# Two-scale attention with a gated convolution: 64-bit weights decoded in other passes and on another engine, one step's coarse scores from raw K, and another opening order

## The chip, the cores and the metric

One core of one Trainium2 chip. The metric is device time in microseconds (us) of one run of the whole program. Engines are named as in the profile: PE (TensorE, matmuls; PEld its weight loads), DVE (VectorE), ACT (ScalarE), POOL (GpSimd), SP (SyncE, which issues most DMAs). Each engine works through its own list of instructions in order, and waits where an instruction's inputs or buffers are not ready.

## The reference

```python
# B=8, H=8, S=576, D=64, factor 4; all in fp32
q_d, k_d, v_d = (mean of 4 neighbours along S of q, k, v)      # 144 rows
out_d  = softmax(q_d k_d^T / 8) v_d                            # coarse attention
out_up = repeat(out_d, 4)
local  = softmax(mask(|i-j| < 4, q k^T / 8)) v                 # banded attention
x = (out_up + local) as (B, S, 512)
# second half: weights come as float64
gate = sigmoid(sum_k conv_w[k] * x shifted by 4-k)             # 5 taps, causal
out  = (gate * (x @ w_val)) @ w_out
```

## The kernel before

**Steps.** The attention runs in 16 steps (`i`), two pairs of heads each (`p = 2i, 2i+1`; 32 pairs in all). A step has these pieces on PE: `sla`, `slb` (local scores, tile `sl`), `sd` (coarse scores), `odp` (coarse weights times V, into tile `x`), `xa`, `xb` (local weights times V, into the same `x`). Between them stand on DVE and ACT: `mx` (row maxima of `sl`), `sub`, `exp`, `sum`, `norm`, `turn` (transpose), `spr` (four copies of 32 partitions into `pt`); for the coarse part `cmx0`, `cexp`, `cnorm`, `cturn`. `oc` copies the coarse result out on ACT, and `xu`, `xt` add both parts into the tile `xt` on DVE.

**Projections.** `xh` and `xl` split `xt` into two parts of fp32r (tiles `xhs`, `xls`), and the product with `w_val` (tile `val`) is made of three matmuls for each of four slices (pieces of 3 matmuls, by blocks `j` of 504 columns). `tap4` and `tap0` to `tap3` make the convolution in tile `gp`, `gate` its sigmoid, `h` the product with `val`; `hhi`, `hlo` split `h` (tile `hhl`), and the product with `w_out` is the tile `out`.

**PSUM.** Scores and `x` share three buffers (`AB`). They are handed round in PE's order: the second `x` tile of step 1 takes the buffer of step 2's `sl`, which `sub` of step 2 frees (line 733).

**Coarse inputs.** For the first two batches (`SUMB`) the sums over 4 neighbours of q and k are made on the chip (`qe`, line 672); later ones by DMAs that add while they land, issued by POOL (`qs`, `vs`, line 585: an issue waits until the one before it has landed). The V sums of the first batch are added from four loads (`vr0` to `vr3`, tiles `vs` and `raw`; `va`, `vc`, `vb`, line 605).

**Weights.** Each of eight chunks (4 of `w_val`, 4 of `w_out`; 128 x 512 float64, tile `raw_v`, `raw_o`) is loaded, then decoded to fp32: three passes on ACT (lines 1007 to 1009), one on DVE (`val`, line 1012), then split into `wh` (ACT, 1036) and `wl` (DVE or POOL, 1039):

```python
nc.scalar.activation(out=low, in_=lo, func=AF.Copy, scale=LOW)                                  # uint16 out
nc.scalar.activation(out=top, in_=hi, func=AF.Prelu, scale=2.0**-40, alpha=2.0**100)            # int16 out
nc.scalar.activation(out=hi, in_=hi, func=AF.Copy, scale=2.0**-112)                             # fp32 out
```

**The order.** A planner in the kernel lists all operations with a cost for each engine that may do them, gives each a due time from PE's order (`tensor_order`), runs a list schedule over these costs, and writes the instructions out in the order of their planned starts. `EARLY` fixes the order of the first loads on SP, `PACE` and `TURN` how PE mixes steps and projections.

Of the kernel before, what the change touches and what calls it, by code (L numbers as in the profile page):

```python
# [12 lines left out]
U16 = mybir.dt.uint16  # L13
# [101 lines left out]
class Transfers:  # L115


    ALONE = {"SP": 0.30, "POOL": 0.16}
    SHARED = {"SP": 0.15, "POOL": 0.128}
    FIRST = {"SP": 1500, "POOL": 1950}  # L120
    LANDING = 1600
# [33 lines left out]
class Planner:  # L155
# [293 lines left out]
def tensor_order():  # L449
# [29 lines left out]
    some("sla slb sd", 0)  # L479
    some("sla slb sd", 1)  # L480
    some("odp xa xb", 0)
    proj(2)
    some("odp xa xb", 1)
    proj(4)
    some("sla slb", 2)
    proj(2)
    some("sd", 2)
    proj(2)
    for s in range(2, NSTEP):
# [10 lines left out]
def tile_two_scale_attn_gated_conv(  # L500
# [183 lines left out]
    def local_scores(i):  # L684
# [315 lines left out]
    def f64_parts(src):  # L1000
# [15 lines left out]
        return fields, value, hi  # L1016

    def weight_chunk(q, nm, w, d):
# [9 lines left out]
        def fields():  # L1028
            t["f"] = f64_parts(t["raw"])
            t["f"][0]()  # L1030

        def value():
            t["f"][1]()
# [8 lines left out]
        op(("fld", q), "ACT", 1700, fields, [("raw", q)])
        op(("val", q), "DVE", 600, value, [("fld", q)], port=ALONE)
        op(("whi", q), "ACT", 530, hi, [("val", q)])
        op(("wlo", q), either(600, 1230), 0, lo, [("whi", q)], port=BOTH)
# [236 lines left out]
```

## Time and profile before

| | |
|---|---|
| median of 3 runs | 375.66 us (374.57 to 375.9) |
| the profiled execution: time, span | 376.08 us, 373.9 us |
| busy: PE, DVE, ACT, POOL | 340.2, 309.7, 251.7, 99.4 us |
| mean granted clock of PE | 0.968 |
| PE busy of 0 to 75 us, of 75 to 300 us | 47.3 us, 222.3 us |

PE's busy time holds the filler matmuls that the kernel puts into gaps (line 558), and runs longer where the granted clock is low. Between span and time lie 2.2 us that are no part of the profile.

### The profile page before, as it was taken

To read this page: it belongs to the slowest core of one execution; us is meant where nothing else is said; L and a number is where in the kernel's file an instruction comes from. 1 tells how busy PE (TensorE), PEld (TensorE's weight loads), DVE (VectorE), ACT (ScalarE), POOL (GpSimd) and SP (SyncE) were. 2 spreads that over 40 slices of the span, in tenths; PEclk is the share of its full clock that TensorE was granted. 3 is DMA by queue.
4 is the path that set the end of the run, shared out by engine and by line. 5 is a ranking of instruction groups with operands and counts; after the bars stand their busy time and mean duration, and the time that the engine had idled before them with its cause. 6 is when DMAs were issued, how large, how long until landed. Compare 5 with 4: busy or idle time off the path is not lost.

```text
span 373.9 us, 12809 instructions
## 1 busy us (share of the span) xinstructions
PE 340.2 (91%) x5517; PEld 266.7 (71%) x5517; DVE 309.7 (83%) x495; ACT 251.7 (67%) x577; POOL 99.4 (27%) x106
## 2 busy tenths in 40 slices
PE   5865725999999899999999999999999999999996
PEld 2644513777777677777777777777777778788996
DVE  6884997999889989999898999998989993937620
ACT  1379998978875779486759694967596667415421
POOL 4223532364033711152035104601450120000000
PEclk9996986799999989999999999999999999999999
DMA  7993899577999899989868996989542301102012
GB/s 220 360 355 141 266 244 309 105 201 199 322 270 273 238 210 225 307 199 246 240 208 237 230 270 163 234 238 255 160 110 85 114 2 57 55 2 85 27 49 79
DMA packets 23463, 70.95 MB, mean 190 GB/s; under 512 B 3184, under 2 KB 9584, under 8 KB 23408
## 3 DMA queue, kind: packets, MB, share of 16 engines
q1 hardware_dynamic: 17504, 52.39, 39.0%
q0 software_dynamic: 5616, 17.50, 26.9%
q8 instruction: 43, 0.70, 0.8%
q10 hardware_dynamic: 288, 0.26, 0.2%
q14 instruction: 12, 0.10, 0.1%
HBM read 60.69 MB, written 9.44 MB: 188 GB/s over the span
## 4 chain that ended last, share of the span: by engine, by line
PE 70%; DVE 17%; ACT 7%; DMA 3%; issue 2%; SPq 0%; DVEq 0%; ACTq 0%
PE out L1058 10%; PE out L1060 8%; PE out L1059 8%; PE val L1058 8%; PE val L1060 7%; PE val L1059 7%; PE x L876 6%; PE x L920 5%; DVE gp L970 5%; PE sd L798 4%; PE sl L706 4%; DMA qk<-in_qk 3%; DVE qs L672 2%; ACT pt L763 1%; PE sl L695 1%
## 5 line engine op out<-in xcount | busy, mean ns | idle before, releaser
L970 DVE SCALAR_TENSOR_TENSOR gp<-xt,cw,gp 128x576 f32<-128x576 f32 x128 | 105.0, 855 | 5.7 <-ACT gp L964 5.4
L1058 PE MATMUL val<-xhs,wh_v 128*128 128x504 f32 (+1 forms) x160 | 63.8, 399 | 6.0 <-ACT xhs L951 6.0
L1060 PE MATMUL val<-xls,wh_v 128*128 128x504 f32 (+1 forms) x160 | 60.5, 378 | 0.8 <-POOL xls L955 0.8
L1059 PE MATMUL val<-xhs,wl_v 128*128 128x504 f32 (+1 forms) x160 | 60.1, 376 | 0.0
L1058 PE MATMUL out<-hhl,wh_o 128*128 128x504 f32 (+1 forms) x144 | 58.6, 407 | 0.0
L1060 PE MATMUL out<-hhl,wh_o 128*128 128x504 f32 (+1 forms) x144 | 55.2, 383 | 0.0
L1059 PE MATMUL out<-hhl,wl_o 128*128 128x504 f32 (+1 forms) x144 | 55.0, 382 | 0.0
L763 ACT COPY pt<-pt 32x576 f32<-32x576 f32 x64 | 42.9, 670 | 9.4 <-PE x L876 4.4
L1106 POOL TENSOR_TENSOR hhl<-h,hhl 128x504 fp32r<-128x504 f32 (+1 forms) x24 | 26.5, 1113 | 79.8 <-ACT hhl L1100 72.3
L1058 PEld LDWEIGHTS val<-xhs,wh_v 128*128 128x128 f32 x160 | 30.6, 191 | 14.3 <-ACT xhs L951 6.3
L891 DVE TENSOR_TENSOR xt<-x,od 128x288 f32<-128x288 f32 x64 | 26.6, 445 | 16.0 <-PE x L876 15.8
L1100 ACT CAST hhl<-h 128x504 fp32r<-128x504 f32 (+2 forms) x44 | 22.2, 519 | 24.6 <-DVE h L1086 24.5
L981 ACT ACTIVATE gp<-gp 128x576 f32<-128x576 f32 x32 | 21.9, 685 | 22.6 <-DVE gp L970 22.0
L1148 ACT ACTIVATE ob<-out 128x504 f32<-128x504 f32 (+2 forms) x40 | 21.7, 553 | 21.4 <-PE out L1060 16.1
L876 PEld LDWEIGHTS x<-pt,vw 64*64 64x64 f32 x1536 | 27.4, 144 | 11.7 <-issue 5.8
L1060 PEld LDWEIGHTS val<-xls,wh_v 128*128 128x128 f32 x160 | 30.4, 190 | 7.0 <-POOL xls L955 1.2
L920 PE MATMUL x<-pdt,vs 32*64 32x145 f32 x640 | 25.5, 294 | 10.2 <-DVE ex L733 7.2
L1059 PEld LDWEIGHTS val<-xhs,wl_v 128*128 128x128 f32 x160 | 30.7, 192 | 4.1
L706 PE MATMUL sl<-qk 128*24 128x60 f32 x1536 | 28.0, 221 | 6.1 <-DMA qk<-in_qk 5.6
L1058 PEld LDWEIGHTS out<-hhl,wh_o 128*128 128x128 f32 x144 | 27.1, 189 | 8.1 <-issue 2.5
L920 PEld LDWEIGHTS x<-pdt,vs 32*64 32x64 f32 x640 | 20.6, 134 | 16.3 <-issue 14.2
L706 PEld LDWEIGHTS sl<-qk 128*24 128x24 f32 x1536 | 25.8, 106 | 8.2 <-issue 4.0
(87 smaller groups left out, 638.7 us busy)
## 6 DMA issues: line engine op xcount, KB each, us to landing
qk<-in_qk SPq DMA_DIRECT2D x64, 291.0 KB, 6.5
vw<-in_vw SPq DMA_DIRECT2D x16, 768.0 KB, 6.0
qs<-in_qkr POOLq DMA_DIRECT2D x18, 576.0 KB, 7.4
out_t<-ob SPq DMA_DIRECT2D x32, 252.0 KB, 4.0
vs<-in_vgr POOLq DMA_DIRECT2D x21, 320.0 KB, 7.5
qs<-in_qkr SPq DMA_DIRECT2D x6, 576.0 KB, 6.7
vs<-in_vgr SPq DMA_DIRECT2D x7, 320.0 KB, 5.4
raw_v<-in_w_val SPq DMA_DIRECT2D x4, 512.0 KB, 7.3
```

Of the source, the lines that this page charges most:

```text
L706: nc.tensor.matmul(out=sc[32 * q : 32 * q + BQ, 2 * KW * g : 2 * KW * (g + 1)].rearrange("p (h k) -> p h k", h=2), lhsT=t[:, 1, 3 + blk : ...
L763: nc.scalar.copy(out=pt2[r, :, q % 2], in_=s["pt"][r, :, 0:BQ])
L876: nc.tensor.matmul(out=s["x", pr][r, part, 0:HALF].rearrange("p (e g j) -> p e g j", e=2, j=BQ)[:, :, g], lhsT=s["vw"][(LO, HI)[pr], n + h ...
L891: nc.vector.tensor_tensor(out=xt, in0=s["x", pr][:, part, 0:HALF].rearrange("p (e j r) -> p e j r", e=2, r=FAC), in1=od.broadcast_to([P, 2 ...
L920: nc.tensor.matmul(out=s["x", q // 2][64 * h : 64 * h + 64, 0, HALF : HALF + NG * CQ].rearrange("p (g j) -> p g j", j=CQ), lhsT=u["vs"][32 ...
L970: nc.vector.scalar_tensor_tensor(out=s["gp"], in0=s["xt"][:, k : k + S], scalar=cw[:, c, k : k + 1], in1=s["gp"], op0=ALU.mult, op1=ALU.add,)
L981: nc.scalar.activation(out=s["gp"], in_=s["gp"], func=AF.Tanh, scale=0.5)
L1058: nc.tensor.matmul(out=o, lhsT=wh[:, d, col], rhs=his[d], start=d == 0, stop=False)
L1059: nc.tensor.matmul(out=o, lhsT=wl[:, d, col], rhs=his[d], start=False, stop=False)
L1060: nc.tensor.matmul(out=o, lhsT=wh[:, d, col], rhs=los[d], start=False, stop=d == NC - 1)
L1100: nc.scalar.copy(out=t["hh"][:, cuts[n]], in_=t["h"][:, cuts[n]])
L1106: eng.tensor_tensor(out=t["hl"][:, cs], in0=t["h"][:, cs], in1=t["hh"][:, cs].bitcast(F32), op=ALU.subtract)
```

## The change

**The decode.** The three ACT passes become three operations of their own. `bits` and `power` write 32-bit words in place and may run on ACT or POOL; `sign` writes the 16-bit field on POOL. In the new order ACT does 14 of these passes over weight chunks, POOL 10.

**Raw K.** With `RAWK = (1,)` the coarse scores of step 1 (`sd`) take K unsummed: four matmuls, one for each of the 4 neighbours, add up in PSUM where one stood (80 instead of 20), and `qe` of pairs 2 and 3 sums 148 outputs instead of 432.

**Who does what.** `qe` may run on POOL as three adds (pairs 1 and 6 do); `spr` and `tap4` may run on POOL (16 of 64 and 9 of 32 do); `tap0` of pairs 0 and 1 becomes a product on ACT (`side`) and an add on POOL. `wl` of two `w_out` chunks goes from POOL to DVE, `cnorm` of two steps from DVE to ACT.

**The order.** `EARLY`, `FIRST` (PE's opening order), `PACE`, the planner's costs, and a table `SHIFT` that moves single due times. There is one buffer fewer for `gp` (`GB` 7).

```diff
-    "qk0 ql0 qk1 ql1 vr0.0:0 vr1.0:0 vr2.0:0 vr3.0:0 vw0 qk2 ql2 qk3 ql3 vr0.1:0 vr1.1:0 vr2.1:0 vr3.1:0 cwf0 raw0 raw1 vw1 raw2 raw3 qk4 ql4 qk5 ql5 vs0.1 raw4 vw2 "
-    "qk6 ql6 raw5 qk7 ql7 raw6 raw7 vw3"
+    "qk0 ql0 qk1 ql1 ql3 vr0.1:0 vr0.0:0 raw0 ql6 qk2 vr1.0:0 vr2.0:0 cwf0 raw1 qk3 ql2 vr1.1:0 vw0 raw2 qk5 vr2.1:0 raw3 qk6 vw1 raw4 vr3.1:0 ql7 raw5 ql5 "
+    "qk7 vr3.0:0 vs0.1 ql4 raw6 vw2 vw3 qk4 raw7"
...
-SUMB, RAWK = 2, ()
+SUMB, RAWK = 2, (1,)
...
-GB = 8
+GB = 7
+SIDE, SIDE2 = 2, 0
...
+FIRST = (
+    "l0 l1 sd0 sd1 p1 p1 p0 x0 p0 p1 p3 odp0 odp1 p1 sd2 l2 x1 p2 p3 p1"
+)
...
+SHIFT = (
+    "tap1:1:1 xl:7:-3 turn:4:6 val:7:1 turn:0:3 qe:5:1 bits:6:3 cturn:4:1 turn:2:6 qe:2:3 sign:5:-6 exp:4:1 sub:0:-20 gate:8:-1 hlo0.0:0:1 sum:2:6 whi:6:1 "
...
+            if lo:
+                half = s["qs"][:, 4 * SD - 2 * n :].rearrange("p (j r) -> p j r", r=2)
+                nc.gpsimd.tensor_tensor(out=half, in0=t[:, :, 0:2], in1=t[:, :, 2:4], op=ALU.add)
+                nc.gpsimd.tensor_tensor(out=out, in0=half[:, :, 0], in1=half[:, :, 1], op=ALU.add)
+                return
+            for r in range(1, FAC):
+                nc.gpsimd.tensor_tensor(out=out, in0=out if r > 1 else t[:, :, :, 0], in1=t[:, :, :, r], op=ALU.add)
...
-            op(k, "ACT", 560, spread(q), [("turn", i)], free=[("xa", i - 1), ("xb", i - 1)])
+            op(k, {"ACT": 680, "POOL": 1250}, 0, spread(q), [("turn", i)], port=("POOL",), free=[("xa", i - 1), ("xb", i - 1)])
...
-        def fields():
-            nc.scalar.activation(out=low, in_=lo, func=AF.Copy, scale=LOW)
-            nc.scalar.activation(out=top, in_=hi, func=AF.Prelu, scale=2.0**-40, alpha=2.0**100)
-            nc.scalar.activation(out=hi, in_=hi, func=AF.Copy, scale=2.0**-112)
+        def scaled(eng, t, by):
+            if eng is nc.scalar:
+                nc.scalar.activation(out=t, in_=t, func=AF.Copy, scale=by)
+            else:
+                eng.tensor_scalar(out=t, in0=t, scalar1=by, scalar2=None, op0=ALU.mult)
+
+        def bits(eng):
+            scaled(eng, lo, LOW)
+
+        def sign():
+            nc.gpsimd.tensor_scalar(
+                out=top, in0=hi, scalar1=0.0, scalar2=-32768.0, op0=ALU.is_lt, op1=ALU.mult
+            )
+
+        def power(eng):
+            scaled(eng, hi, 2.0**-112)
```

Two places in the program show the new order. Lines of the new kernel differ from those of the old: `qe` 690, `xu`/`xt` 918, `mx` 755, `cmx0` 835, `sub` 760, `sum` 769, `turn` 783, `cturn` 875, `wl` 1097, `xl` 984, V sums 622, `sign` 1062, `bits` and `power` 1056, `spr` 790, `norm` 776.

On DVE, in front of `sub` of step 2 (`ex<-sl_533` before, `ex<-sl_545` now); before:

```order
L848 STREAM_TRANSPOSE pdt_656<-pd 128x800
L1012 SCALAR_TENSOR_TENSOR raw_v_334<-raw_v_334 128x512
L970 SCALAR_TENSOR_TENSOR gp_630<-xt_82,cw,gp_630 128x576
L970 SCALAR_TENSOR_TENSOR gp_653<-xt_83,cw,gp_653 128x576
L1039 TENSOR_TENSOR wl_v<-raw_v_334,wh_v 128x512
...
L733 TENSOR_TENSOR ex<-sl_533,mx_621 128x24x30
```

and now, from the first add into `xt` of step 0 (tiles `xt_82`, `xt_83`) on:

```order
L918 TENSOR_TENSOR xt_82<-x_0_502,od_0_575 128x2x144
L783 STREAM_TRANSPOSE pt_670<-ex 128x768
L918 TENSOR_TENSOR xt_82<-x_0_502,od_0_575 128x2x144
L918 TENSOR_TENSOR xt_83<-x_0_503,od_0_579 128x2x144
L690 TENSOR_REDUCE qs_674<-qk_81 128x432
L918 TENSOR_TENSOR xt_83<-x_0_503,od_0_579 128x2x144
L755 TENSOR_REDUCE mx_714<-sl_545 128x24
L835 TENSOR_REDUCE cmx_720<-sd_684 128x5
L760 TENSOR_TENSOR ex<-sl_545,mx_714 128x24x30
```

The taps (line 970), seven of them, and the work on the weight chunk stood ahead of `sub`; now `sub` follows the adds into `xt`, one sum, and two row maxima, and all taps stand behind it.

On POOL, from the second chunk's `wl` to the split of step 0's `xt`; now (before, `wl`, `wl`, `xls`, `xls` stood here with nothing between):

```order
L1056 TENSOR_SCALAR raw_v_248<-raw_v_248 128x512
L1062 TENSOR_SCALAR raw_v_248<-raw_v_248 128x512
L1056 TENSOR_SCALAR raw_v_248<-raw_v_248 128x512
L1062 TENSOR_SCALAR raw_v_264<-raw_v_264 128x512
L622 TENSOR_TENSOR vs_123<-vs_123,raw_3_313 128x320
L622 TENSOR_TENSOR vs_123<-vs_123,raw_3_437 128x320
L602 DMA vs_449<-in_vgr 128x640
L776 TENSOR_TENSOR ex<-ex,rs_466 128x24x30
L1097 TENSOR_TENSOR wl_v<-raw_v_248,wh_v 128x512
L1097 TENSOR_TENSOR wl_v<-raw_v_264,wh_v 128x512
L698 TENSOR_TENSOR qs_674<-qk_80 128x432
L984 TENSOR_TENSOR xls<-xt_82,xhs 128x576
```

The passes over the third and fourth chunk, two of the V sums, `norm` of step 1 and the sums of pair 6 have come in ahead of `xls`, which the first product waits for. (Between the last two rows stand two more adds like the one on `qs_674`.)

## Rows read from the trace of the kernel before

**Rows 1.** Busy time by stretch: length, busy us (instructions), granted clock, DMA share, GB/s.
```profile
core 0: us, PE busy (x) PEld busy (x) DVE busy (x) ACT busy (x) POOL busy (x), PEclk, DMA share, GB/s
18.70:28.00 9.30, 5.72 (x96) 3.78 (x94) 7.75 (x12) 6.70 (x11) 2.06 (x3) 1.00 0.97 356
28.00:37.40 9.40, 5.19 (x121) 3.76 (x120) 4.43 (x8) 9.31 (x22) 3.33 (x2) 0.64 0.36 141
46.70:56.00 9.30, 2.57 (x29) 1.71 (x29) 9.30 (x13) 8.56 (x10) 3.02 (x3) 0.85 0.93 242
65.40:75.00 9.60, 9.18 (x126) 6.96 (x127) 8.86 (x15) 9.54 (x18) 3.98 (x5) 0.74 0.59 103
75.00:300.00 225.00, 222.28 (x3983) 171.97 (x3983) 210.29 (x345) 165.09 (x407) 71.15 (x70) 0.99 0.80 217
```

**Rows 2.** Timeline of PE to 84 us: start, length, line, tile, count [idle before <-releaser].
```profile
32.34 1.33 PE L558 MATMUL x<-const-bfloat16-1.0 128*128 128x350 bf16 x4 [4.21 <-ACT od L933]
...
33.59 2.79 PE L876 MATMUL x<-pt,vw 64*64 64x48 f32 x96
...
44.43 1.43 PE L798 MATMUL sd<-qs 128*32 128x144 f32 x40
...
55.21 2.68 PE L920 MATMUL x<-pdt,vs 32*64 32x145 f32 x36 [6.73 <-DVE ex L733]
...
58.88 2.16 PE L876 MATMUL x<-pt,vw 64*64 64x48 f32 x96
...
65.82 0.79 PE L1058 MATMUL val<-xhs,wh_v 128*128 128x504 f32 x1 [4.78 <-ACT xhs L951]
...
70.90 0.39 PE L1058 MATMUL val<-xhs,wh_v 128*128 128x504 f32 x1
...
83.08 0.49 PE L1058 MATMUL out<-hhl,wh_o 128*128 128x504 f32 x1
```

**Rows 3.** Timeline of DVE, 36 to 55 us.
```profile
36.50 1.55 DVE L891 TENSOR_TENSOR xt<-x,od 128x288 f32<-128x288 f32 x4 [2.13 <-PE x L876]
...
48.46 1.53 DVE L970 SCALAR_TENSOR_TENSOR gp<-xt,cw,gp 128x576 f32<-128x576 f32 x2
...
50.52 3.72 DVE L970 SCALAR_TENSOR_TENSOR gp<-xt,cw,gp 128x576 f32<-128x576 f32 x5
...
54.17 0.89 DVE L733 TENSOR_TENSOR ex<-sl,mx 128x720 f32<-128x720 f32 x1
```

**Rows 4.** ACT by form: the three passes over a weight chunk; mean ns.
```profile
L1007 ACT ACTIVATE raw_v<-raw_v 128x512 uint16<-128x512 uint32 x4 | 5.5, 1366 | 0.0
...
L1008 ACT ACTIVATE raw_v<-raw_v 128x512 int16<-128x512 f32 x4 | 5.4, 1360 | 0.1
...
L1009 ACT ACTIVATE raw_v<-raw_v 128x512 f32<-128x512 f32 x4 | 2.7, 669 | 0.1
```

**Rows 5.** Chain that ended last: the wait for the last part of step 1's scores data.
```profile
9.55 7.32 DMA qk<-in_qk
```

**Rows 6.** Tile raw_v on POOL: ns min/median/max.
```profile
L1039 POOL TENSOR_TENSOR wl_v<-raw_v,wh_v x3: 1294/1297/2077, 33.5 to 46.7; 128x512 fp32r<-128x512 f32 x3
```

**Rows 7.** POOL by form, mean ns.
```profile
L605 POOL TENSOR_TENSOR vs<-vs,raw 128x320 f32<-128x320 f32 x3 | 2.6, 863 | 2.3 <-DVE vs L605 2.2
...
L955 POOL TENSOR_TENSOR xls<-xt,xhs 128x432 fp32r<-128x432 f32 x1 | 1.1, 1140 | 0.0
...
L545 POOL MEMSET pt<- 128x1152 f32 x1 | 1.1, 1061 | 0.0
```

**Rows 8.** DVE by form, mean ns.
```profile
L672 DVE TENSOR_REDUCE qs<-qk 128x432 f32<-128x1728 f32 x8 | 15.4, 1942 | 1.9 <-DMA qk<-in_qk 1.9
```

**Rows 9.** Timeline of DVE and of POOL from 224 us, and DVE at 257.84 us.
```profile
224.40 4.01 DVE L970 SCALAR_TENSOR_TENSOR gp<-xt,cw,gp 128x576 f32<-128x576 f32 x4
...
225.37 1.70 POOL L1106 TENSOR_TENSOR hhl<-h,hhl 128x504 fp32r<-128x504 f32 x1 [11.33 <-ACT hhl L1100]
...
257.84 2.28 DVE L970 SCALAR_TENSOR_TENSOR gp<-xt,cw,gp 128x576 f32<-128x576 f32 x3 [0.70 <-ACT gp L964]
```

More of the change, by code (lines that the diff above doesn't have):

```diff
@@ L115 @@
 class Transfers:
[L118 to L121, printed above, removed]
+    ALONE = {"SP": 0.37, "POOL": 0.16}
+    SHARED = {"SP": 0.20, "POOL": 0.11}
+    FIRST = {"SP": 1200, "POOL": 1950}
+    LANDING = 1400
     def __init__(self):
@@ L168 @@
     ISSUE = {"SP": 620}
-    BEGIN = {"SP": 700, "ACT": 2450, "PE": 600, "POOL": 3000}
+    BEGIN = {"SP": 1500, "ACT": 2450, "PE": 600, "POOL": 3000}
     WINDOW = 14
@@ L252, in rank @@
             ops[k]["due"] = due
+        for word in SHIFT.split():
+            name, i, by = word.split(":")
+            if (name, int(i)) in ops:
+                ops[name, int(i)]["due"] += 1000 * int(by)
     def simulate(self):
@@ L338, in pick @@
             best = None
-            for due, k in sorted(ready[e]):
+            line = ready[e]
+            if e == "DVE":
+                line = [(due + LEAVE * ("POOL" in ops[k]["opts"]), k) for due, k in line]
+            for due, k in sorted(line):
                 if k in start or at[k].get(e, 0) > now:
@@ L477, in goal @@
                 return int(m + (n - m) * (t - a) / (b - a))
[L479 to L489, printed above, removed]
+    for word in FIRST.split():
+        name, i = word.rstrip("0123456789"), int(word.lstrip("abcdefghijklmnopqrstuvwxyz"))
+        if name == "p":
+            proj(i)
+        else:
+            some({"l": "sla slb", "x": "xa xb"}.get(name, name), i)
+    for s in range(TURNS, NSTEP):
         seen = 0
@@ L657, in pool, with add @@
         s = st[p]
-        def add():
+        def add(eng):
             u = at[p // 2]
@@ L1014, in value @@
             )
-        return fields, value, hi
+        return bits, sign, power, value, hi
     def weight_chunk(q, nm, w, d):
@@ L1026, in dma, with step, run @@
             nc.sync.dma_start(out=t["raw"], in_=w[:, d])
[L1028 to L1033, printed above, removed]
+        def step(n):
+            def run(*eng):
+                if "f" not in t:
+                    t["f"] = f64_parts(t["raw"])
+                t["f"][n](*eng)
+            return run
         def hi():
-            nc.scalar.copy(out=wh, in_=t["f"][2])
+            nc.scalar.copy(out=wh, in_=t["f"][4])
         def lo(eng):
-            eng.tensor_tensor(out=wl, in0=t["f"][2], in1=wh.bitcast(F32), op=ALU.subtract)
+            eng.tensor_tensor(out=wl, in0=t["f"][4], in1=wh.bitcast(F32), op=ALU.subtract)
         op(("raw", q), "SP", 620, dma, free=[("wlo", q - RAWB)], size=P * 512 * 8)
[L1042 to L1045, printed above, removed]
+        op(("bits", q), {"ACT": 600, "POOL": 1300}, 0, step(0), [("raw", q)], port=("POOL",))
+        op(("sign", q), "POOL", 1350, step(1), [("bits", q)], port=("POOL",))
+        op(("power", q), {"ACT": 580, "POOL": 1300}, 0, step(2), [("sign", q)], port=("POOL",))
+        op(("val", q), "DVE", 600, step(3), [("power", q)], port=ALONE)
+        op(("whi", q), "ACT", 560, hi, [("val", q)])
+        op(("wlo", q), either(600, 1300), 0, lo, [("whi", q)], port=BOTH)
         whl[nm, d] = ("wlo", q)
```

74 lines of the change are left out of this document (50 added, 24 removed), and 6 rows, old and new, of the table SHIFT.

## Prediction

> **What bounds the kernel now.** I read the busy time by stretch first. From 75 to 300 us PE is busy for 222.3 of 225 us at a granted clock of 0.99 [rows 1]: PE is the bound there, and this change takes no matmul out of it. Before 75 us it is busy for 47.3 us of 75 (the table above). So what can be won lies in the opening: how early PE comes to the point from which it never starves. As that point I take the first matmul of `val_2` of block 0, at 70.90 us [rows 2]; the PE work behind it is the same matmuls before and after.
>
> The timeline of PE then names the waits on the way there [rows 2]. The first `xa` waits 4.21 us for `oc` on ACT, until 32.34. `odp` of step 1 gets its first four matmuls out and waits 6.73 us, until 55.21, for DVE's `ex` (line 733): that is `sub` of step 2, which frees the PSUM buffer. The third piece of `val_0` waits 4.78 us for `xhs`, until 65.82. The timeline of DVE shows why `sub` came so late: seven taps stand ahead of it, from 48.46 to 54.2 [rows 3], while DVE is busy for all of 46.7 to 56 us and PE for 2.57 us [rows 1]. ACT is full from 28 to 37.4 us (9.31 of 9.4) and from 65.4 to 75 [rows 1], and 27 us of its opening are passes over weights: 8 chunks x (1.37 + 1.36 + 0.67) [rows 4].
>
> **The change part by part.** *The decode.* A pass that writes 16-bit fields takes 1.36 us on ACT, one that writes 32-bit words of the same count 0.67 [rows 4]. I price `bits` (it now writes uint32) at 0.67; its bounds are 0.67 and 1.37, since the only row with an integer output is a 16-bit one. ACT is left with 14 passes, 9.4 us in place of 27: 18 us less. [...]
>
> POOL gets 10 passes over weight chunks. No row has its one-input arithmetic; the nearest is a two-input 128x512 operation, 1.29 us [rows 6]. Its memset (128x1152 in 1.06 us) [rows 7] gives 0.5 us as the lower bound; for the upper bound of `sign`, which writes 16 bits, I double the 1.29 as ACT's rows do [rows 4]: 2.6. I take 1.3, the row of the same tile and the same steps.
>
> *Sums.* `qe` costs DVE 1.94 us a pair [rows 8]. Two pairs go to POOL, as three adds of 432 elements each at 1.14 [rows 7], 3.4 us (bounds 3.4 and, since the row is of unit step and these step by four words, twice that); two shrink to a third (0.7 us). DVE saves 6.4 us. [...]
>
> *Raw K* makes `sd` of step 1 four times 1.43 us [rows 2], 4.3 us more on PE. It lies in the stretch 18.7 to 37.4 us where PE was busy for 10.9 of 18.7 [rows 1], and its result is needed only by `odp` of step 1, 10 us later. I cost it at nothing; uncovered it would cost 4.3.
>
> *The opening, station by station.* I follow the new order with the durations of the trace.
>
> (a) Loads. Bytes by tile shapes: 0.298 MB for a `qk` half, 0.786 for `vw`, 0.524 for a weight chunk, 0.164 for a V part. Before, the last piece of step 1 landed at 16.87 [rows 5] with 4.01 MB queued up to it, and the queue moved 356 GB/s until 28 us [rows 1]. Now `vr3.0`, the last V part, stands at 8.16 MB: 16.87 + 4.15/0.356 = 28.5 us. The last half of step 2's `qk` stands at 9.61 MB: 32.6 us. Until then no load waits for a buffer that is still in use.
>
> (b) `odp` of step 0 needs `vb`: an add on POOL (0.86 [rows 7]) and one on DVE (some 0.5) behind 28.5, so 30; 1.5 us on PE, then `oc` until 32, as before (32.03 to 32.34). The passes no longer hold `oc`, but the V load does.
>
> (c) In PE's list the first half of step 2's `sl` stands ahead of `xa`: 32.6 + 0.7. `xa`, `xb` then take 2.8 as before [rows 2]: done at 36.1, where it was 36.4. So far almost nothing is won.
>
> (d) DVE behind it: four adds into `xt` (1.55 together [rows 3]), a transpose (0.9), one `qe` (1.9), `mx`, `cmx0` and `sub` (0.85 each, by the row of `sub` [rows 3]): 43.0. Before, `sub` ended at 55.06 [rows 3]. This is the main term, 12 us: `qe` of step 2 and `cturn` of step 1 now run while DVE waits for `xa`, and taps and weight work stand behind `sub`.
>
> (e) `odp` of step 1 is also queued behind the first piece of `val_0`, which needs `xls` from POOL. POOL: chunk 3 lands at 21.8 (5.77 MB queued); three passes and the `sign` of chunk 4, 5.2; the V adds wait for 28.5 and end at 29.4; a DMA issue and `norm` of step 1, 2.5: 31.9. ACT has `wh` of chunks 3 and 4 done at 33.6 and 34.2, behind `oc` at 32.5; so the two `wl` end at 36.3, three adds at 39.7, `xls` (1.5) at 41.2; the piece 0.7 and fillers 0.6 give 42.5. DVE's 43.0 decides, by 0.5 us. `odp` then takes 1.5 to 2.7: 45.2.
>
> (f) Three pieces (2.1 to 3.3) and `xa`, `xb` (1.6 to 2.8) of step 1: 50.1, before 61.04 (58.88 + 2.16 [rows 2]). Adds into `xt` 0.8, two taps 1.5 and two `xls` 1.4 on DVE, with ACT's `xhs` beside the taps: the third piece of `val_0` can run at 53.8. Before it was 65.82, 12.0 us later; ACT no longer has a chunk's three passes here.
>
> (g) Four pieces more, 2.8 at full clock or 5.1 as before (65.82 to 70.90): 56.6 to 58.9 against 70.90. The gain here is 12 to 14 us.
>
> *Given back.* What DVE had done by 70.90 and now has not is about 5 us: three chunks' `val`, two `wl`, a tap, an `hlo`. From 53.8 on it has ten taps (0.76 each [rows 9]), two `h`, four `val`, two `wl` and one step's softmax pieces ahead of the first `hlo`: 18.4 us, so 72.2. PE's own work up to the first `out` piece was 12.2 us (70.90 to 83.08 [rows 2]) and now holds step 4's `sl` too (1.5): it ends at about 71.4. So `out_0` starts at 72.2, where it was 83.08 [rows 2]: 10.9 us earlier, and with 1.5 us less of PE work behind it. From there PE is the bound as before.
>
> **Sum.** 376.08 - 10.9 - 1.5 = 363.7 us for the profiled execution, which stood 0.4 above the median of the runs shown; I say 364, since a chain worked out in whole pieces leaves out small waits.
>
> **Rivals.**
> *GpSimd holds the opening* (0.16). If `sign` costs 2.6 us, four of them ahead of station (e) put 5.2 us on POOL; if the strided adds cost double, 3.4 more. Less the 0.5 of slack, the first piece of `val_0` comes 2.8 to 8 us later and `sub` no longer decides; likeliest 5: 367 to 371. For it: POOL had nothing but 0.9 and 1.3 us pieces in the opening and is now in front of both the V sums and `xls`. Against it: the strided weight reads of `wl` ran at 1.29 already.
>
> *The loads come later* (0.10). (a) takes 356 GB/s on to 33 us; from 46.7 to 56 us the old kernel got 242 [rows 1], with POOL's adding loads in the queue. At 242 GB/s beyond 28 us the `qk` of step 2 would land at 34.8, and with SP held at one buffer for some us more, PE follows by 4 to 6: 368 to 370.
>
> *Given back in the middle* (0.14), the one that can end on the other side. POOL and DVE slow each other: four taps took 4.01 us beside one POOL operation of 1.70, where three took 2.28 without [rows 9], so about 1 us lost. Behind the opening POOL now has 16 copies and 9 `tap4` more, and a few splits less. DVE idles for 14.7 us of the 225 [rows 1]. If half of the 25 fall beside taps, it loses 12 us, which the idle time covers. Slower than before needs 27 us lost (12.4 and the 14.7), over 1 us for each of the 25 with all 25 beside taps; that gives 378 to 381 (0.06). Between lies 370 to 377 (0.08). Against it: POOL was busy for 71 us of that stretch before, and PE starved for 2.7 [rows 1].
>
> **How the numbers follow.** The main case has 0.58 and 360 to 367: its low end is no hand-back beyond PE's own work (0.8 us) and full clock in (e) to (g) (2.5), its high end `bits` at 1.37 us (half of 5 us on the path). A change that wins nothing, because a wait that I didn't follow takes the place of `sub`'s, gets 0.02. Over 372 lie the middle's 0.14 less a third and the upper ends of the first two rivals; with what lies under 359.5 this makes 0.2, so the range is 359.5 to 372. A measurement of this kernel tells changes of over 0.5% (1.9 us) from none. Slower by that: 0.06. Within: 0.06 (half of the middle's 0.08, and the 0.02). Faster: 0.88.
>
> **What would show it.** Right: no wait of PE for `ex` above 2 us in `odp` of step 1, which starts at 41 to 46 us; `val_2` of block 0 before 60 us; `out_0` 10 to 12 us earlier; 222 of 225 us busy behind it. `bits` at 0.67 on ACT and POOL's passes at 0.6 to 1.4. Wrong: `sign` over 2 us, `odp` of step 0 later than 33, or PE waits for `h`, `hhl` or `pt` of over 5 us in sum behind 90 us.

## Result and profile after

| | before | after |
|---|---|---|
| median (runs) | 375.12 us (4) | 370.11 us (4; 368.78 to 371.32) |
| ratio, 95% interval | | 0.9844 [0.9801, 0.9886] |
| profiled execution: time, span | 376.08, 373.9 us | 368.78, 367.0 us |
| busy: PE, DVE, ACT, POOL | 340.2, 309.7, 251.7, 99.4 us | 344.0, 305.0, 221.9, 156.3 us |

The time fell by 1.6%, on the side and in the range that were forecast, 6 us above the forecast itself: outside the main case (360 to 367) and inside the times of the rival "GpSimd holds the opening" (367 to 371). A second measurement of the same kernel gave 0.9839 (`again`, below). Busy time by stretch of the kernel after, in the columns of [rows 1]:

```profile
18.70:28.00 9.30, 8.30 (x172) 5.36 (x165) 8.77 (x15) 7.95 (x21) 8.98 (x5) 1.00 1.03 404
28.00:37.40 9.40, 6.02 (x89) 3.72 (x85) 5.97 (x7) 3.90 (x16) 8.10 (x6) 1.00 0.66 196
46.70:56.00 9.30, 7.30 (x153) 5.23 (x151) 7.54 (x13) 9.15 (x25) 7.62 (x6) 1.00 1.02 337
56.00:65.40 9.40, 7.71 (x72) 5.46 (x73) 9.40 (x12) 7.18 (x15) 9.33 (x6) 0.82 0.82 198
65.40:75.00 9.60, 9.60 (x235) 7.13 (x236) 9.28 (x14) 7.18 (x19) 6.04 (x5) 1.00 0.62 141
75.00:100.00 25.00, 21.44 (x362) 16.30 (x354) 22.86 (x39) 17.60 (x47) 11.44 (x11) 0.93 0.93 232
75.00:300.00 225.00, 220.63 (x3884) 170.35 (x3878) 211.43 (x355) 152.33 (x393) 91.39 (x88) 0.99 0.80 216
```

PE now works for 7.30 us of 46.7 to 56, where it had 2.57 [rows 1], and starves later: of 75 to 100 us it works for 21.4 (24.7 before), at a granted clock of 0.93 (1.00 before). POOL is full from 18.7 to 28 us and from 56 to 65.4; DVE is full from 56 to 75. The timeline of PE of the kernel after:

```profile
20.42 10.56 PE L825 MATMUL sd<-qk,qs 128*32 128x144 f32 x160 [0.99 <-DVE qs L690]
36.59 1.51 PE L947 MATMUL x<-pdt,vs 32*64 32x145 f32 x40 [3.38 <-DVE vs L622]
...
48.96 1.45 PE L947 MATMUL x<-pdt,vs 32*64 32x145 f32 x36 [0.23 <-DVE ex L760]
...
56.28 0.49 PE L1118 MATMUL val<-xhs,wh_v 128*128 128x504 f32 x1 [2.05 <-ACT xhs L980]
...
63.48 0.49 PE L1118 MATMUL val<-xhs,wh_v 128*128 128x504 f32 x1 [0.36 <-DVE h L1146]
...
81.48 1.21 PE L575 MATMUL out<-const-bfloat16-1.0 128*128 128x350 bf16 x6 [2.46 <-DVE h L1146]
82.27 0.85 PE L1118 MATMUL out<-hhl,wh_o 128*128 128x504 f32 x1
```

The wait for `ex` is 0.23 us instead of 6.73, the third piece of `val_0` runs at 56.28 instead of 65.82, `val_2` at 63.48 instead of 70.90 [rows 2]. But the first `out` matmul stands at 82.27, 0.8 us before its old place, because PE waits for an `h`. Behind that wait the granted clock (the third number from the end) stood at 0.56 and 0.58 for 4 us, in which most `out` matmuls started 0.42 us apart, against 0.23 from 86 us on at 1.00. I estimate from the shares that this costs some 1.7 us more (0.44 and 0.42 of two times 2 us):

```profile
82.00:84.00 2.00, 2.00 (x8) 1.23 (x7) 2.00 (x5) 1.04 (x4) 1.62 (x3) 0.56 1.08 215
84.00:86.00 2.00, 2.00 (x7) 1.61 (x6) 2.00 (x6) 1.75 (x5) 0.28 (x1) 0.58 1.04 207
```

The timeline of DVE of the kernel after:

```profile
31.06 0.91 DVE L835 TENSOR_REDUCE cmx<-sd 128x5 f32<-128x720 f32 x1 [3.21 <-PE sd L825]
...
34.20 1.95 DVE L857 TENSOR_SCALAR cs<-csm 128x5 f32<-128x5 f32 x1 [0.37 <-ACT pd L845]
36.06 0.48 DVE L622 TENSOR_TENSOR vs<-vs,raw 128x320 f32<-128x320 f32 x1
...
47.92 0.90 DVE L760 TENSOR_TENSOR ex<-sl,mx 128x720 f32<-128x720 f32 x1
...
59.05 2.00 DVE L1009 SCALAR_TENSOR_TENSOR gp<-xt,cw,gp 128x576 f32<-128x576 f32 x2
...
78.45 0.68 DVE L1166 TENSOR_TENSOR hhl<-h,hhl 128x504 fp32r<-128x504 f32 x1
79.04 1.80 DVE L1009 SCALAR_TENSOR_TENSOR gp<-xt,cw,gp 128x576 f32<-128x576 f32 x1
80.77 0.67 DVE L1146 SCALAR_TENSOR_TENSOR h<-gp,val 128x504 f32<-128x504 f32 x1
```

This `h` is `h_2`. It frees the `val` buffer that `out_0` takes (two buffers, tag "v"), and on DVE it stands behind `hlo_0` and a tap. Groups of POOL up to 75 us and of ACT, with their mean ns, of the kernel after:

```profile
L1062 POOL TENSOR_SCALAR raw_v<-raw_v 128x512 int16<-128x512 f32 x4 | 11.7, 2918 | 1.7 <-ACT raw_v L1054 1.2 <-ACT cbi L839 0.4
L1062 POOL TENSOR_SCALAR raw_o<-raw_o 128x512 int16<-128x512 f32 x4 | 11.5, 3007 | 0.0
L698 POOL TENSOR_TENSOR qs<-qs,qk 128x432 f32<-128x432 f32 x4 | 5.3, 1326 | 0.3
L1056 POOL TENSOR_SCALAR raw_v<-raw_v 128x512 uint32<-128x512 uint32 x1 | 1.6, 1583 | 0.1
```

```profile
L1054 ACT ACTIVATE raw_o<-raw_o 128x512 uint32<-128x512 uint32 x4 | 2.6, 672 | 0.1
```

So `bits` costs ACT 0.67 us as priced; `sign` costs POOL 2.9 to 3.0 us and `bits` 1.58, where 1.3 was taken for either.

**Where the 6.9 us of the span came from.** `sl` of step 5 starts at 102.36 us before and 100.57 after, `sl` of step 15 at 291.07 and 284.56. So 1.8 us were won before 100 us, 4.7 between steps 5 and 15, 0.4 behind. Groups of PE from 102.36 to 291.07 us of the kernel before:

```profile
L876 PE MATMUL x<-pt,vw 64*64 64x48 f32 x960 | 19.0, 224 | 0.5 <-DVE xt L891 0.5
L920 PE MATMUL x<-pdt,vs 32*64 32x145 f32 x400 | 15.1, 285 | 1.4 <-DVE pdt L848 1.0 <-DVE ex L733 0.4
L558 PE MATMUL val<-const-bfloat16-1.0 128*128 128x350 bf16 x8 | 1.5, 314 | 0.1
```

and the windows behind the 1.4 us wait (columns as in [rows 1]; the granted clock is the third number from the end):

```profile
128.00:130.00 2.00, 0.80 (x6) 0.19 (x4) 2.00 (x4) 1.53 (x3) 0.80 (x1) 1.00 1.03 243
130.00:132.00 2.00, 1.81 (x38) 1.54 (x39) 2.00 (x4) 1.96 (x4) 0.00 (x0) 0.95 0.98 211
132.00:134.00 2.00, 2.00 (x6) 1.29 (x4) 2.00 (x4) 1.76 (x8) 0.86 (x1) 0.50 0.91 204
134.00:136.00 2.00, 2.00 (x51) 1.70 (x51) 1.05 (x3) 1.68 (x7) 0.47 (x1) 0.69 0.86 152
```

After, the same stretch (100.57 to 284.56) has no filler matmuls, no wait of `x`, and 0.8 us of waits in all. Before: 1.5 us of fillers, 2.5 us of waits (of them the 0.5 and the 1.4 here), and 1.7 us lost to the clock by the same estimate, as it stood at 0.95, 0.50 and 0.69 behind the wait (0.05, 0.50 and 0.31 of three times 2 us). That is 1.5 + 1.7 + 1.7 = 4.9 against the 4.7 measured. It is the account of one pair of executions; `b_sub` below shows another.

### The profile page after: what moved, and what is told of

It is laid out like the page before. It is cut to its first block, busy times and chain, and to the rows that moved or that the text cites. A ratio compares the mean times of both kernels' runs of the same rounds, so it can differ in the third digit from the quotient of the medians.

```text
span 367.0 us, 13034 instructions
## 1 busy us (share of the span) xinstructions
PE 344.0 (94%) x5625; PEld 268.3 (73%) x5625; DVE 305.0 (83%) x495; ACT 221.9 (60%) x553; POOL 156.3 (43%) x144
## 4 chain that ended last, share of the span: by engine, by line
PE 82%; DVE 11%; DMA 3%; issue 2%; ACT 1%; SPq 1%; DVEq 0%; ACTq 0%
PE out L1118 11%; PE val L1118 10%; PE out L1120 9%; PE out L1119 9%; PE val L1120 8%; PE val L1119 8%; PE sd L825 7%; PE x L903 7%; PE x L947 6%; PE sl L733 4%; DVE gp L1009 4%; DMA qk<-in_qk 2%; DMA vw<-in_vw 2%; PE sl L722 1%; DVE xt L918 1%
## 5 line engine op out<-in xcount | busy, mean ns | idle before, releaser
L790 ACT COPY pt<-pt 32x576 f32<-32x576 f32 x48 | 32.2, 670 | 10.6 <-PE x L903 5.4
L1166 POOL TENSOR_TENSOR hhl<-h,hhl 128x504 fp32r<-128x504 f32 (+2 forms) x21 | 23.8, 1154 | 32.1 <-ACT hhl L1160 32.1
L602 POOL DMA_DIRECT2D vs<-in_vgr x21 | 19.8, 942 | 32.8 <-DMA vs<-in_vgr 32.5
L903 PEld LDWEIGHTS x<-pt,vw 64*64 64x64 f32 x1536 | 26.0, 138 | 10.4 <-issue 7.5
L1160 ACT CAST hhl<-h 128x504 fp32r<-128x504 f32 (+2 forms) x44 | 21.8, 518 | 18.6 <-DVE h L1146 18.5
L1146 DVE SCALAR_TENSOR_TENSOR h<-gp,val 128x288 f32<-128x288 f32 (+6 forms) x64 | 26.4, 443 | 6.4 <-PE val L1120 6.2
```

What stands on the lines that cost most here:

```text
L790: (nc.scalar.copy if eng is nc.scalar else eng.tensor_copy)(out=pt2[r, :, q % 2], in_=s["pt"][r, :, 0:BQ])
L903: nc.tensor.matmul(out=s["x", pr][r, part, 0:HALF].rearrange("p (e g j) -> p e g j", e=2, j=BQ)[:, :, g], lhsT=s["vw"][(LO, HI)[pr], n + h ...
L1146: nc.vector.scalar_tensor_tensor(out=t["h"][:, cs], in0=st[b * NC + c]["gp"][:, f:e], scalar=1.0, in1=box["o"][:, cs], op0=ALU.add, op1=AL ...
L1166: eng.tensor_tensor(out=t["hl"][:, cs], in0=t["h"][:, cs], in1=t["hh"][:, cs].bitcast(F32), op=ALU.subtract)
```

## Experiments

Theory A: the opening lost what it lost because `sign` on POOL costs 2.9 us instead of 1.3. Theory B: because raw K holds PE for 10.56 us and DVE waits for it. Theory C: DVE's list from the split of step 0 to `h_2` is full, `out_0` waits for its end, and what is won before 60 us ends there. All ratios are to the kernel before on the same chip.

**The same kernel again (`again`).**

> The changed kernel itself, as the reference point of this set. Both theories: 369 to 371 us, odp of step 0 at 36.6 us, val_2 of block 0 at 63.5, out_0 at 82.3.

370.52 us, 0.9839 [0.9771, 0.9906]; `odp` of step 0 at 35.73, `h_2` at 81.50, `sl` of step 5 at 101.31. Two traces of one kernel thus differ by 0.7 to 0.9 us at these points: the guard that took 1.95 us in the first took 0.36 here.

**A cheaper sign (`sign32`): a 32-bit word, over the low word.** Three bits of the weights are lost.

```diff
-                out=top, in0=hi, scalar1=0.0, scalar2=-32768.0, op0=ALU.is_lt, op1=ALU.mult
+                out=lo.bitcast(F32), in0=hi, scalar1=0.0, scalar2=0.0, op0=ALU.min, op1=ALU.mult
```

> sign on GpSimd writes one 32-bit word over the low word instead of a 16-bit field; the weights lose the three lowest of their mantissa bits; order unchanged. Theory A (the 2.7 us passes of sign on GpSimd hold the opening and slow VectorE's taps beside them): a pass falls to about 1.55 us, as the 32-bit passes on GpSimd took, xls and the V sums come 3 to 4 us earlier, h_2 of block 0 4 us earlier, 366 to 367 us. Theory B (the 10.6 us of step 1's scores on raw K hold VectorE's list, and through it odp of step 0): odp of step 0 stays at 36 to 37 us and the time falls by under 1.5 us.

368.89 us, 0.9794 [0.9720, 0.9868]. The pass cost 2.14 us on `raw_v` and 2.98 on `raw_o`, not 1.55. `odp` of step 0 came at 33.71, 2.0 us before `again` on the same chip (2.9 before the kernel after); `h_2` at 79.94, 1.6 us before `again` (0.8). Theory A wanted 4 us at `h_2`.

**K read in one piece (`k_contig`)**, so that other columns are added up:

```diff
-.rearrange("p (j r) -> p j r", r=FAC)[:, :, r]
+.rearrange("p (r j) -> p j r", r=FAC)[:, :, r]
```

> Step 1's scores read K in four contiguous runs instead of every fourth column, so other columns are summed; shapes, counts and order unchanged. If the step of the read is what made the 160 matmuls take 10.6 us, they take 5.5 to 6 here. Theory B: VectorE's guard for step 1 and odp of step 0 come 2 us earlier at least, val_2 of block 0 at 59 to 61, 366 to 368 us. Theory A: odp of step 0 still waits for GpSimd's V adds, at 34 us, and the time falls by under 1 us.

368.90 us, 0.9805 [0.9733, 0.9876]. The group of `sd` of step 1 on PE, first of the kernel after, then of this one:

```profile
L825 PE MATMUL sd<-qk,qs 128*32 128x144 f32 x160 | 10.6, 438 | 1.0 <-DVE qs L690 1.0
```

```profile
L825 PE MATMUL sd<-qk,qs 128*32 128x144 f32 x160 | 5.8, 296 | 1.4 <-issue 1.4
```

The step of four words in the read nearly doubled the matmuls' time (10.56 us); without it they take 5.8, about the 5.7 us that were predicted. `odp` of step 0 came at 33.77, 2.0 us before `again`: DVE's `cmx0`, which waited 3.21 us for `sd` in the kernel after, waited 1.20. `h_2` stood at 81.42, where it was.

**Both (`sign32_kc`).**

> Both edits at once: sign in 32 bits, contiguous K (wrong columns summed, three mantissa bits lost). If A and B each hold part of the opening side by side, odp of step 0 starts at 30 to 31 us, val_2 of block 0 at 57 to 59, and the time is 363 to 365, more than the two single gains together. If what VectorE does behind 60 us decides (theory C), the early points move by 5 us and the end by under 2: 368 us.

367.88 us, 0.9757 [0.9675, 0.9840]; `odp` of step 0 at 34.10, `h_2` at 80.53. The two long operations together moved `h_2` by under 1 us, and the 2.0 us that each alone gave `odp` did not add up. That speaks against A and B as the main cause; the intervals of these three kernels and of `again` overlap.

**The sign back on ACT (`sign_act`).**

```diff
-            nc.gpsimd.tensor_scalar(
-                out=top, in0=hi, scalar1=0.0, scalar2=-32768.0, op0=ALU.is_lt, op1=ALU.mult
-            )
+            nc.scalar.activation(out=top, in_=hi, func=AF.Prelu, scale=2.0**-40, alpha=2.0**100)
```

> After's order, with the sign of the weights written by ACT again (1.36 us a pass, as in the kernel before) and nothing of it on GpSimd. Theory A (the price of sign on GpSimd, 2.9 us in place of 1.3, is what the opening lost): odp of step 0 at 33 to 34 us, first out matmul at 77 to 78, 365 to 366 us. Theory C (DVE's list between the xls of pair 0 and h_2 is full, about 25 us, and out_0 waits for h_2): h_2 ends at 79 to 81, only the slowing of taps beside the signs goes (about 1 to 1.5 us), 368 to 369 us. Rival: ACT, with 13.6 us of passes back in the opening, holds xhs and oc again: third piece of val_0 later than 60 us, 371 or more.

368.83 us, 0.9821 [0.9774, 0.9868]: C's time, and no more than 1.7 us from the kernel after, which its interval does not tell apart. `odp` of step 0 came at 34.09, the third piece of `val_0` at 56.15, where it was. POOL, then DVE of this kernel:

```profile
78.70 0.88 POOL L602 DMA_DIRECT2D qs<-in_qkr  x1 [6.89 <-DMA qs<-in_qkr]
79.31 1.56 POOL L1164 TENSOR_TENSOR hhl<-h,hhl 128x504 fp32r<-128x504 f32 x1
```

```profile
64.11 1.01 DVE L875 STREAM_TRANSPOSE pdt<-pd 128x800 f32<-128x800 f32 x1 [2.01 <-ACT pd L869]
...
78.39 0.81 DVE L1009 SCALAR_TENSOR_TENSOR gp<-xt,cw,gp 128x576 f32<-128x576 f32 x1
80.90 0.68 DVE L1144 SCALAR_TENSOR_TENSOR h<-gp,val 128x504 f32<-128x504 f32 x1 [1.70 <-POOL hhl L1164]
```

DVE's taps are no longer slowed (0.81 us in the mean from 56 to 82 us, 1.00 in the kernel after), and `h_2` still stands at 80.90: it starts as POOL's `hlo_1` ends, which stood behind the issue of an adding load that had waited 6.89 us for its forerunner to land. Whether DVE was held by POOL's operation itself or by a semaphore, the profile does not say. With this and the 2.01 us for ACT's `pd` DVE had gaps, so C holds here only as far as `out_0` waits for `h_2`: that DVE's list is full is so in the kernel after, not in this one.

**Pooled sums again (`act_rawkoff`)**: `sign_act` with `RAWK` without effect.

```diff
-            lo, n = (1, CQ * (NG - 1) + 32) if p // 2 in RAWK else (0, 3 * SD)
+            lo, n = 0, 3 * SD
...
-                for r in range(planes):
+                for r in range(1):
...
```

> sign_act with step 1's coarse scores on pooled sums again: qe of pairs 2 and 3 whole (two times 1.94 us on DVE in place of 0.75), sd of step 1 in 1.43 us in place of about 10.5. In the prediction raw K cost nothing. If so: 368.5 to 370, odp of step 0 within 0.5 us of sign_act's 34.1. If its 9 us on PE and the wait of DVE for it hold odp of step 0: odp of step 0 at 31 to 32.5, xa of step 0 3 us earlier or up to the landing of the last V part and step 2's loads; by theory C no more than 1 us of it is left at h_2: 367.5 to 368.5.

368.70 us, 0.9782 [0.9732, 0.9832]. PE of this kernel:

```profile
21.98 1.43 PE L825 MATMUL sd<-qs 128*32 128x144 f32 x40 [0.32 <-DVE qs L690]
...
33.74 2.69 PE L947 MATMUL x<-pdt,vs 32*64 32x145 f32 x40 [8.12 <-DVE vs L622]
```

`sd` is done 7 us sooner and PE waits 8.12 us for the V sum instead. `odp` of step 0 moved by 0.35 us: the pooled sums, longer by 2.4 us on DVE, take the place of DVE's wait for `sd`. So against pooled sums raw K costs nothing, and Theory B falls as the cause of the time. What raw K takes beyond its price does cost 2 us at `odp` of step 0 (`k_contig`), which is gone at `h_2`.

**POOL's copies and `tap4` on ACT (`pool_off`).**

```diff
-                (nc.scalar.copy if eng is nc.scalar else eng.tensor_copy)(out=pt2[r, :, q % 2], in_=s["pt"][r, :, 0:BQ])
+                nc.scalar.copy(out=pt2[r, :, q % 2], in_=s["pt"][r, :, 0:BQ])
...
-            if eng is nc.scalar:
+            if True:
```

> After's order, with the spread copies and the tap4 operations that GpSimd has taken over put on ACT at the same places of the program. If they are what won the about 5 us between 100 and 200 us (they relieve ACT there): 373 to 376 us, PE waits for pdt, ex or pt in 120 to 142 us as before. If they cost by slowing DVE: 366 to 368. If neither (ACT is busy for 60% of the span and has room): 369.5 to 371.

370.85 us, 0.9867 [0.9824, 0.9909]: within the error of the kernel after. Steps 5 to 15 took 185.28 us, 1.3 more than after and 3.4 less than before. So the gain of the middle is in the main not these copies.

**The main term alone (`b_sub`)**: the kernel before, with these of DVE moved behind `slb` of step 2, ahead of the taps:

```diff
...
+        move = [("qe", 4), ("qe", 5), ("mx", 2), ("sub", 2)]
...
```

> The kernel before, with DVE's qe, mx and sub of step 2 moved ahead of the seven taps, and nothing else. The main term alone: sub of step 2 ends at 47 to 49 us (before 55.06), odp of step 1 by 49. If what ends the opening is PE's chain from odp of step 1, out_0 comes 3 to 6 us earlier: 370 to 373 us. Theory C (DVE's whole work up to h_2 sets out_0; order inside it moves nothing): 374.5 to 377, first out matmul within 1.5 us of 83.08.

374.34 us, 0.9958 [0.9918, 0.9999]. `sub` ended at 44.5 us, 10.6 earlier. PE of this kernel:

```profile
57.99 1.04 PE L565 MATMUL x<-const-bfloat16-1.0 128*128 128x350 bf16 x3 [8.45 <-ACT od L940]
...
83.83 0.49 PE L1065 MATMUL out<-hhl,wh_o 128*128 128x504 f32 x1
```

The 6.73 us wait for `ex` [rows 2] became one of 8.45 us for `od`, which stands behind six weight passes on ACT; `out` starts 0.75 us later than before. `sl` of step 5 stands at 103.37 and of step 15 at 288.37: 185.00 us between them in the order of the kernel before, 3.7 less than there and no more than in `pool_off`.

**The same with `bits` in 32-bit words (`b_sub_bits`).**

```diff
-            nc.scalar.activation(out=low, in_=lo, func=AF.Copy, scale=LOW)
+            nc.scalar.activation(out=lo, in_=lo, func=AF.Copy, scale=LOW)
```

> The kernel before with b_sub's order on DVE and bits as 32-bit words on ACT (0.67 in place of 1.36 us), sign and power on ACT as before: no pass on GpSimd, no raw K, no new order elsewhere. In b_sub the gain of sub went into a wait of 8.45 us for od of step 1, behind ACT's weight passes. If those passes are what holds it: od of step 1 4 to 5 us earlier (57.7 to about 53), third piece of val_0 at 61 to 63 (66.35 in b_sub), first out matmul at 79.5 to 81.5, 369 to 372 us. Theory C with DVE full from there: third piece as said, out_0 no earlier than 82, 372 to 374.5.

373.88 us, 0.9912 [0.9873, 0.9952]. PE of this kernel:

```profile
55.18 1.03 PE L565 MATMUL x<-const-bfloat16-1.0 128*128 128x350 bf16 x3 [7.12 <-ACT od L940]
...
81.67 0.49 PE L1065 MATMUL out<-hhl,wh_o 128*128 128x504 f32 x1
```

`od` came 2.8 us sooner, the third piece of `val_0` at 63.72, and `sl` of step 5 at 100.70: what the whole change has there (100.57). `out_0` is a little earlier than C gave it (82) and later than the other forecast (81.5); the time is C's. Behind step 5 this kernel and `b_sub` keep the 1.4 us wait of `x` and the eight fillers of the kernel before; this one takes 188.08 us up to step 15.

**The decode alone (`b_decode`)**: the kernel before with 32-bit `bits` on ACT and `sign` on POOL.

> The kernel before, in its own order, with the decode alone: bits as 32-bit words on ACT (0.67 in place of 1.37 us), sign on GpSimd (2.7 to 3 us) instead of ACT (1.36 us), the power still on ACT. ACT loses 2.06 us a chunk. If ACT's passes held the opening (the 4.2 us wait for oc, the 4.8 us for xhs): out_0 2 to 5 us earlier, 371 to 374 us. If GpSimd's longer passes come in the way of xls and wl: out_0 later than 83, 376 to 380. If DVE's list sets it (theory C): within 1.5 us of before.

383.01 us, 1.0177 [1.0121, 1.0232]: slower, beyond all three forecasts. ACT of this kernel:

```profile
27.44 0.65 ACT L1011 ACTIVATE raw_v<-raw_v 128x512 f32<-128x512 f32 x1 [2.78 <-POOL raw_v L1008]
31.43 0.65 ACT L1011 ACTIVATE raw_v<-raw_v 128x512 f32<-128x512 f32 x1 [2.76 <-POOL raw_v L1008]
```

ACT's third pass waits 2.76 to 3.35 us for POOL in each of the seven chunks from 26 to 72 us, with `od` and `xhs` queued behind it. The new order puts other work of ACT between the passes, and there this costs 2.5 us in all on `raw_v`.

**`h_2` first (`h2_first`)**: `sign_act` with single operations moved, each behind another:

```diff
...
+            (("tap3", 2), ("tap2", 2)), (("gate", 2), ("cexp4", 3)),
+            (("hlo0.0", 0), ("hhi1.0", 0)), (("h2", 0), ("hlo0.0", 0)), (("hlo1.0", 0), ("h2", 0)),
+            (("hhi2.0", 0), ("hlo1.0", 0)), (("tap1", 3), ("hhi2.0", 0)), (("hlo2.0", 0), ("tap2", 3)),
...
```

> sign_act (after's order with sign on ACT), with h_2 and what it needs brought forward: the last taps of pair 2, its gate, hlo_0 and h_2 now stand ahead of the three last taps of pair 3 on DVE, and hlo_1 on GpSimd ahead of the accumulating loads it stood behind. In sign_act h_2 ended at 81.6 us and PE waited for it. Theory C (out_0 waits for h_2, that is for DVE's list): h_2 ends at 77.5 to 78.5, the first out matmul is at 78 to 79.5 instead of 83.1, then PE waits for hlo_3, which moves by 1 to 2 us only; sl of step 5 at 98 to 99.5 (100.5 in sign_act), 366.5 to 368 us. Rival (the opening is no longer what decides; the middle takes any gain back): h_2 earlier, but sl of step 6 within 0.5 us of sign_act's 119.6, 368.5 to 369.5.

367.24 us, 0.9756 [0.9695, 0.9817]. PE of this kernel:

```profile
78.59 1.08 PE L584 MATMUL out<-const-bfloat16-1.0 128*128 128x350 bf16 x6
...
83.10 0.46 PE L584 MATMUL out<-const-bfloat16-1.0 128*128 128x350 bf16 x2 [2.75 <-DVE h L1153]
...
121.45 0.47 PE L1125 MATMUL out<-hhl,wh_o 128*128 128x504 f32 x1 [1.14 <-DVE h L1153]
```

`h_2` started at 77.63, `out_0` at 78.59 without a wait, `sl` of step 5 at 98.97: C as expected (this profiled run took 370.41 us, the other three 366.96 to 367.27). But a wait for `h_3` stands next, and one for an `h` of block 1 at 121 us; `sl` of step 7 is at 138.04, where the kernel after has 137.98, so in this trace the rival's case holds two steps on. And the clock stood at 1.00 from 75 to 100 us here, where the kernel after had 0.93 and `sign_act` 0.86: by my estimate from these shares (0.07 of 25 us) that alone is as much as the 1.6 us won at step 5.

**And PE's list (`h2_pe`)**: `h2_first` with the first two pieces of `out_1` behind the second and third of `out_0`.

```diff
...
+            (("o1.0", 0), ("o0.2", 0)), (("o1.1", 0), ("o1.0", 0)),
...
```

> h2_first with one more move, on PE: the first two pieces of out_1 (whose PSUM buffer h_3 frees) now stand behind the second and third piece of out_0, which need only hlo_1 and hlo_2. In h2_first PE waited 2.75 us there for h_3 with these two pieces behind the wait. If PE's list is what holds out_0 and what is won stays won: sl of step 5 at 97 to 98 us (98.97), 365.5 to 366.5 us. If DVE, busy for 23.5 of 25 us from 75 to 100 us and 39.1 of 42 to 142, takes it back (PE waited 2.0 us for h of block 1 in h2_first): sl of step 5 as said, but sl of step 6 no earlier than 118, 366.8 to 367.8 us.

368.23 us, 0.9840 [0.9798, 0.9882], above both forecasts. PE, then the windows of this kernel:

```profile
121.47 0.46 PE L1126 MATMUL out<-hhl,wh_o 128*128 128x504 f32 x1 [1.90 <-DVE h L1154]
```

```profile
120.00:142.00 22.00, 20.53 (x339) 15.80 (x340) 21.97 (x41) 18.08 (x49) 8.54 (x10) 1.00 0.82 218
```

The wait for `h_3` fell to 0.93 us, but `sl` of step 5 stayed at 98.92 and the wait in block 1 grew to 1.90, with DVE busy for 21.97 of 22 us (21.96 in the kernel after); `sl` of step 7 is at 138.05. What PE wins by 100 us is gone by 138, in a stretch in which DVE is full. The intervals of `h2_first`, `h2_pe` and the kernel after overlap: no version is shown to beat it.

## Why the prediction came out as it did

**Where it failed.** The step is the given-back: "From 53.8 on it has ten taps ... ahead of the first `hlo`: 18.4 us, so 72.2 ... So `out_0` starts at 72.2". Its length was right: from 59.05 to `hlo_0` at 78.45 are 19.4 us. Its start was 5.25 us late, and `out_0` waits not for `hlo_0` but for `h_2`, 3.0 us behind it, a PSUM buffer that I had not followed. 72.2 + 5.25 + 1.0 + 3.0 = 81.45, where PE's wait ended (81.48). `h2_first` shows that the place is right: with `h_2` early the wait is gone. The signs show it too: `sign` over 2 us and `odp` of step 0 later than 33 were named for a wrong forecast and came; `val_2` of block 0 before 60 us, named for a right one, did not (63.48).

**Why 59.05 and not 53.8.** Stations (a) to (d): POOL's passes ran from 23.49 to 32.2, where I had 5.2 us from 21.8 on, up to 27.0, at 1.3 each; the V adds had no load to wait for and started behind them at 32.01. On DVE the V add stood in order behind `cmx0`, which raw K held up to 31.06, `qe` and the guard of step 1's softmax, which took 1.95 us for 128x5 beside POOL. My station (b) had looked at the V load and at POOL alone. So `odp` of step 0 came at 36.59 instead of 30, `xa`, `xb` ended at 41.9 instead of 36.1, `sub` at 48.8 instead of 43.0. From the end of `xb` to `sub` are 6.9 us in both: the main term had its size, at a later place. `act_rawkoff` shows the DVE part by itself: its V adds on POOL ended at 30.9, DVE's came at 33.21, behind `qe` and the guard. Of step (e), the 0.23 us left of the wait for `ex` is right.

**Why the time was still near.** `out_0` won 0.8 us in place of 10.9, and 1.8 instead of 12.4 at step 5. "From there PE is the bound as before" failed to the other side: 5.1 us were won behind 100 us, in this pair of traces with fewer waits, no fillers and no fall of the clock there. So that the time fell into the range is in part luck: a gain in the opening that was 10.6 us short, and 5.1 us behind it that no term of mine held. In `after`, `sign_act` and `pool_off`, all of the new order, the 1.4 us wait is gone, in `b_sub` and `b_sub_bits`, of the old one, it stands as before. But how much of the 5.1 us the order gives is not shown. The fall of the clock is not in each run of the old order: in `b_sub` and `b_sub_bits` the same 1.4 us wait passed at 1.00. And from step 5 to 15 the old order took 188.71, 185.00 and 188.08 us (before, `b_sub`, `b_sub_bits`), the new one 183.99, 183.82 and 185.28 (`after`, `sign_act`, `pool_off`), but 187.19 in `h2_first`: the order saves 1 us against `b_sub` and 4 against `b_sub_bits`, which starts this stretch where `after` does. The order of that stretch alone was not run.

**The rivals.** "GpSimd holds the opening" gave 367 to 371 and its mark, `sign` over 2 us, came true, above even its bound of 2.6. It is a cause of the late stations, but without it (`sign_act`) only 1.3 to 1.7 us come back, and these lie within the error. Nor was it right in its mechanism: the strided adds did not double, and `sub` still decided, as the 0.23 us wait for `ex` shows. "Loads come later" fell: the V adds waited for none. "Given back in the middle" was there already ahead of the middle, as taps of 1.0 us in the mean from 56 to 82 us, 0.81 in `sign_act`; in the middle itself `pool_off`, without POOL's copies, was no faster, so it did not decide. DVE was longer beside POOL here too: the 128x5 guard took 1.95 us, against 0.16 at 96.82 us with POOL idle, and it ended at 36.15, POOL's `norm` at 36.11:

```profile
34.46 1.65 POOL L776 TENSOR_TENSOR ex<-ex,rs 128x720 f32<-128x720 f32 x1
```

**Single prices.** `bits` at 0.67 was right: the 32-bit words of the row [rows 4] cost half of the 16-bit fields (0.67 against 1.36), and `bits` in 32-bit words took 0.67. The strided adds on POOL took 1.24 and 1.33, near the 1.14 of the row; the factor two of their upper bound was my guess, and no run shows it. `bits` and `power` on POOL 1.55 to 1.58, above the 1.4 that I allowed. Raw K 10.56 in place of 5.7: costing it at nothing was wrong by 2 us for `odp` of step 0 (`k_contig`) and right for `h_2`.

## What to carry to other kernels

Follow each stage to all that it waits for, the buffer that it takes as much as its inputs: here the input, `hlo_0`, was there 2.3 us before the buffer. Where two engines are nearly full (PE 98%, DVE 94% of 75 to 300 us), an order that relieves one hands the time on to the next wait, so a gain in a stage counts only when the steps behind it are still earlier: in `h2_first` 1.6 us at step 5 were gone at step 7. Read on which engine an operation stands in line before pricing what it needs.

## What the hardware showed that was not expected

- A matmul whose moving fp32 operand steps by four words took 438 ns a record and 66 ns of pace (10.56 us for 160), against 296 and 36 ns in one piece (5.8 us for 160, `k_contig`). Why it does is not shown.
- POOL's one-input pass over 128x512 with 16-bit output and two operations on each element took 2.9 to 3.0 us in the mean, the 32-bit pass with one operation 1.55 to 1.58, a two-input operation of that size 1.31. With two operations and a 32-bit output (`sign32`, `raw_v`) it took 2.14, so the narrow output is not the whole of it. On ACT the 16-bit pass took 1.36 against 0.67.
- The guard, an operation of 128x5 on DVE, took 1.95 us (kernel after) and 0.44 us (`act_rawkoff`) beside `norm` on POOL and ended within 0.04 us of it both times (36.15 and 36.11, 33.29 and 33.26). It took 0.16 us alone (96.82 us), but as little beside POOL's one-input `bits` pass (24.17 us): it is not longer beside every operation of POOL.
